# A causal attention kernel with a gated linear unit: convolution on sixteen 32x32 tiles for two groups at once, 64-column projection tiles, and a start written out piece by piece

## The chip, the cores and the metric

The kernel runs on one core of one Trainium2 chip. The metric is the device time of one execution in microseconds (us), as the median of several runs; a profiled execution additionally gives a trace, whose span is about 2 us shorter than the timed value. Runs are called fast or slow: a run is slow when it is over 1.5% above the fastest run of the same kernel, and only fast runs enter the ratios. PE is the TensorE matmul engine, DVE the VectorE, ACT the ScalarE, POOL the GpSimd, SP the SyncE.

## The reference, cut to what matters

```python
q, k, v: (8, 12, 448, 64)                       # batch, heads, positions, head width
scores = q @ k.T / 8, masked above the diagonal
x = softmax(scores) @ v  ->  (8, 448, 768)      # heads side by side
gate = sigmoid(sum over t of conv_w[t] * x shifted by 4 - t positions)    # 5 taps, causal, per channel
out  = (gate * (x @ w_val)) @ w_out             # both 768 x 768
```

The kernel works on groups of four heads, three groups per batch, 24 in all. It writes the sigmoid as (1 + tanh(z/2))/2, so ACT needs one set of functions.

## The kernel before: the parts that the change touches

A half of a group's scores is 16 matmuls with 32 rows each, four row tiles of the array side by side. ACT turns it into exponentials, POOL masks the diagonal, the attention matmuls (32 columns each, four column tiles) follow, DVE normalizes into `x`, and the convolution multiplies `x` with 32x32 diagonal matrices, one per tap:

```python
def conv(n):                                     # one group
    for t in range(KW):                          # 5 taps
        for dh in range(2):
            for i in range(G):                   # 4 heads
                j = 2 * (i % 2) + dh
                r = slice(32 * i, 32 * (i + 1))
                nc.tensor.matmul(out=av_ps[i // 2][32 * j:32 * (j + 1), 0:S], lhsT=cwd[r, 2 * g + dh, t],
                                 rhs=x[r, dh, t:t + S], ..., tile_position=(32 * i, 32 * j))
    # then two tanh activations of 448 columns, from av_ps
def val(b, g, o):       # 6 matmuls of 128x128 per tile: x @ w_val, then gate * value on DVE
def project(p, m, half, o):   # 6 x 4 matmuls of 128x32: (gate * value) @ w_out, then a copy and a store
...
for n in range(N + 1):
    load_v(n + 2)
    scores(n, 0); softmax_numerators(n, 0)
    attend(n - 1); normalize(n - 1)
    next_out(limit, z_ps); next_out(limit, den_ps)       # output tiles fill in
    scores(n, 1); softmax_numerators(n, 1)
    conv(n - 1); transposes(n + 1); cast_v(n + 1); load_qk(n + 3)
    ...                                                  # w_val is loaded in step 0, w_out in steps 1 and 2
    val(b - 1, g, (den_ps, z_ps))
```

Eight of the array's sixteen 32x32 tiles work in a convolution. Everything is in program order; there are eight PSUM banks: four for scores, two for attention (`av`), one for denominators (`den`), one free (`z`).

The softmax here doesn't subtract the row's maximum and nothing guards it: scores larger than these inputs give would overflow.

## Time and profile before

| | before |
|---|---|
| time, median of 3 runs | 240.46 us (239.91 to 240.92) |
| span of the profiled run | 238.6 us |
| PE busy | 211.0 us, 88% |
| PE's first value tile | 36.76 us |
| steady period | 7.95 us per group |

The page's busy shares, slices, stretches and chain are shown and read in the prediction below.

### The profile page before, as it was taken

What the parts mean: (1) busy time and instruction counts of PE and PEld (TensorE: products, weight loads), DVE (VectorE), ACT (ScalarE), POOL (GpSimd) and SP (SyncE); (2) the same over time, 40 slices, a digit from 0 to 9 for tenths busy, and PEclk for the clock granted to TensorE, in tenths of its full rate; (3) what the DMA queues carried; (4) which work ended last, traced back from release to release, by engine and by line L of the source; (5) the groups of instructions that cost most, each with busy time, mean ns of one, the idle gap of its engine ahead of it and who ended that gap; (6) DMA issues with size and microseconds to landing.
All of it is one profiled execution on the core that took longest, in us unless ns stands there. A gap on an engine that the chain in (4) does not pass through costs nothing.

```text
span 238.6 us, 10214 instructions
## 1 busy us (share of the span) xinstructions
PE 211.0 (88%) x4518; PEld 117.1 (49%) x4518; DVE 138.1 (58%) x235; ACT 143.1 (60%) x201; POOL 110.7 (46%) x189
## 2 busy tenths in 40 slices
PE   0297389988988999999999999999999999999893
PEld 0154145554544555545554555555555555544462
DVE  3457466754776678657766776586678663622100
ACT  2367543488765677668676867776777677231241
POOL 7594795153746535733655365347534532100000
PEclk9999859999999999999999999999999999999999
DMA  6999999959795568787768876877797111111153
GB/s 124 225 192 161 191 217 206 176 145 213 152 203 111 103 147 163 156 189 166 145 152 209 180 121 162 235 154 155 184 191 140 41 69 69 69 65 70 69 201 132
DMA packets 59574, 36.07 MB, mean 151 GB/s; under 512 B 48261, under 2 KB 55941, under 8 KB 59530
## 3 DMA queue, kind: packets, MB, share of 16 engines
q0 software_dynamic: 10944, 13.38, 35.4%
q1 hardware_dynamic: 48586, 22.04, 35.0%
q8 instruction: 35, 0.57, 1.0%
q14 instruction: 9, 0.07, 0.1%
HBM read 37.76 MB, written 11.01 MB: 204 GB/s over the span
## 4 chain that ended last, share of the span: by engine, by line
PE 77%; DMA 9%; POOL 3%; DVE 3%; issue 3%; ACT 3%; SPq 0%; POOLq 0%; DVEq 0%
PE den_ps L230 11%; PE z_ps L230 10%; PE av_ps L214 9%; PE z_ps L248 9%; PE sc_ps L154 9%; PE av_ps L187 8%; DMA kb<-in_k_dram 7%; PE den_ps L248 7%; PE sc_ps L248 5%; PE den_ps L187 5%; PE av_ps L230 2%; ACT ob L250 2%; ACT pt L163 1%; DMA vf<-in_v_dram 1%; DVE x L200 1%
## 5 line engine op out<-in xcount | busy, mean ns | idle before, releaser
L163 ACT ACTIVATE pt<-sc_ps 128x1024 bf16<-128x1024 f32 x96 | 93.0, 1021 | 50.4 <-PE sc_ps L154 49.1
L173 POOL TENSOR_SCALAR_AFFINE_SELECT pt<-pt 128x512 bf16<-128x512 bf16 x48 | 29.6, 642 | 59.3 <-ACT pt L163 48.4
L154 PE MATMUL sc_ps<-qt,kt 32*128 32x448 bf16 (+3 forms) x768 | 35.0, 285 | 17.7 <-DVE kt L140 13.4
L248 PEld LDWEIGHTS <-gv 128*32 128x32 bf16 x1344 | 35.3, 97 | 20.1 <-issue 5.3
L230 PEld LDWEIGHTS <-wv 128*128 128x128 bf16 x288 | 26.4, 98 | 30.4 <-issue 8.1
L154 PEld LDWEIGHTS <-kt 32*128 32x128 bf16 x768 | 17.4, 96 | 41.9 <-DVE kt L140 14.7
L232 DVE SCALAR_TENSOR_TENSOR gv<-gate,den_ps 128x448 bf16<-128x448 f32 x22 | 13.7, 621 | 32.5 <-ACT gate L219 22.6
L214 PE MATMUL av_ps<-x,cwd 32*32 32x448 bf16 x960 | 29.8, 349 | 2.3 <-DVE x L200 2.2
L200 DVE TENSOR_TENSOR x<-av_ps,rb 128x448 bf16<-128x448 f32 x48 | 27.7, 620 | 3.1
L230 PE MATMUL den_ps<-x,wv 128*128 128x448 bf16 x132 | 28.8, 354 | 0.0
L230 PE MATMUL z_ps<-x,wv 128*128 128x448 bf16 x132 | 28.6, 352 | 0.0
L76 POOL CAST vb<-vf 128x1024 bf16<-128x1024 f32 x24 | 24.9, 1037 | 6.7 <-DMA vf<-in_v_dram 6.7
L248 PE MATMUL z_ps<-wo,gv 128*32 128x384 bf16 x576 | 27.6, 326 | 0.0
L167 POOL TENSOR_SCALAR_AFFINE_SELECT pt<-pt 128x512 bf16<-128x512 bf16 x24 | 15.4, 642 | 25.6 <-ACT pt L163 25.6
L194 DVE STREAM_TRANSPOSE dt<-den_ps 128x448 f32<-128x448 f32 x24 | 15.6, 650 | 19.9 <-PE den_ps L187 19.9
L140 DVE STREAM_TRANSPOSE qt<-qb 128x448 uint32<-128x448 uint32 x24 | 22.9, 952 | 7.0 <-DMA qb<-in_q_dram 7.0
L187 PE MATMUL av_ps<-pt,vb 128*32 128x448 bf16 (+3 forms) x768 | 26.7, 283 | 0.0
L219 ACT ACTIVATE gate<-av_ps 128x448 f32<-128x448 f32 x48 | 23.7, 555 | 1.1 <-PE av_ps L214 0.8
L140 DVE STREAM_TRANSPOSE kt<-kb 128x448 uint32<-128x448 uint32 x24 | 22.4, 934 | 2.5 <-DMA kb<-in_k_dram 2.5
L248 PE MATMUL den_ps<-wo,gv 128*32 128x384 bf16 x456 | 21.9, 326 | 0.0
L187 PEld LDWEIGHTS <-vb 128*32 128x32 bf16 x768 | 17.2, 101 | 6.0 <-issue 0.8
L250 ACT ACTIVATE ob<-z_ps 128x384 f32<-128x384 f32 x24 | 11.8, 491 | 13.3 <-PE z_ps L248 13.3
(36 smaller groups left out, 161.7 us busy)
## 6 DMA issues: line engine op xcount, KB each, us to landing
out_dram<-ob SPq DMA_DIRECT2D x28, 384.0 KB, 3.4
vf<-in_v_dram SPq DMA_DIRECT2D x72, 128.0 KB, 4.5
qb<-in_q_dram POOLq DMA_DIRECT2D x24, 224.0 KB, 3.9
kb<-in_k_dram POOLq DMA_DIRECT2D x24, 224.0 KB, 5.1
vf<-in_v_dram SPq DMA_DIRECT2D x24, 64.0 KB, 3.7
wv<-in_moe_w_val_dram POOLq DMA_DIRECT2D x6, 192.0 KB, 10.6
wo<-in_moe_w_out_dram POOLq DMA_DIRECT2D x6, 192.0 KB, 8.2
cwn<-in_moe_conv_w_dram SPq DMA_DIRECT2D x1, 15.0 KB
```

Of the source, the lines that this page charges most:

```text
L76: nc.gpsimd.tensor_copy(out=t, in_=vfs.pop(n))
L140: nc.vector.transpose(out=t.bitcast(U32).rearrange("p (b s) -> p s b", s=T), in_=qks.pop((name, n)).rearrange("p s d -> p (s d)").bitcast( ...
L154: nc.tensor.matmul(out=sc_ps[h // 2][:, h % 2, c0:c0 + nq], lhsT=kt[r, e, k0:k0 + 128], rhs=qt[r, e, q0:S], start=e == 0, stop=e == 1, ski ...
L163: nc.scalar.activation(out=pt[:, 2 * hp:2 * hp + 2, 512 * stage:512 * (stage + 1)], in_=sc_ps[hp], func=AF.Exp, scale=D ** -0.5)
L173: nc.gpsimd.affine_select(out=pt[:, :, c:c + 128], in_=pt[:, :, c:c + 128], compare_op=ALU.is_ge, fill=0.0, base=0, pattern=[[0, G], [1, 1 ...
L187: nc.tensor.matmul(out=o, lhsT=w, rhs=pt[:, h, col:col + nq], start=i == 0, stop=i == 3, skip_group_check=True, tile_position=(0, 32 * h))
L200: nc.vector.tensor_tensor(out=x[:, dh, 4:S + 4], in0=av_ps[dh][:, 0:S], in1=r, op=ALU.mult)
L214: nc.tensor.matmul(out=av_ps[i // 2][32 * j:32 * (j + 1), 0:S], lhsT=cwd[r, 2 * g + dh, t], rhs=x[r, dh, t:t + S], start=t == 0, stop=t == ...
L219: nc.scalar.activation(out=gate[:, e], in_=av_ps[e][:, 0:S], func=AF.Tanh, scale=0.5)
L230: nc.tensor.matmul(out=o[e][:, 0:S], lhsT=wv_sb[c][:, f:f + 128], rhs=xs[(NG * b + cg) % 8][:, ce, 4:S + 4], start=c == 0, stop=c == NE - ...
L248: nc.tensor.matmul(out=o[r, 0:384], lhsT=gvs[p][g][:, dh, 128 * m + 32 * j:128 * m + 32 * (j + 1)], rhs=wo_sb[c][:, f], start=c == 0, stop ...
L250: nc.scalar.activation(out=ob[:, f], in_=o[:, 0:384], func=AF.Copy, scale=0.5)
```

## The change

The intent: use the eight idle array tiles for a second group (half the convolution waves), give the value and output matmuls a shape that lets the second group come out with its 64-row halves exchanged (64-column tiles; w_out is kept a second time with halves exchanged), order the groups 0 1 2 2 0 1 over two batches so that pairs fit, and write the first eight groups out as a list of tokens, so that the head of the run can be interleaved by hand. The diff, cut to its core:

```diff
+ORDER = [(b + d, g) for b in range(0, B, 2) for d, g in ((0, 0), (0, 1), (0, 2), (1, 2), (1, 0), (1, 1))]
+PROLOGUE = """
+K1 K0 Lq.0 Lv.0 Lk.0 Lq.1 Lk.1 Lv.1 K3 Lq.2 Lk.2 K2 Lv.2 K4 Tq.0 Lv.3 K5 Tk.0 Tq.1 s.0.0.0 Tk.1 s.0.0.1
+E.0.0.0 E.0.0.1 s.0.1.0 Tq.2 E.0.1.0 s.0.1.1 M.0.0 M.0.1 Tk.2 E.0.1.1 s.1.0.0 Lq.3 V.0 Lk.3 E.1.0.0 s.1.0.1
 ...
+s.3.1.0 D.2 N.1.2 E.3.1.0 s.3.1.1 M.3.0 N.2.0 M.3.1 N.1.3 E.3.1.1 s.4.0.0 W.0 N.2.1 W.1 N.1.4 E.4.0.0 s.4.0.1
+W.2 N.2.2 W.3 E.4.0.1 V.2 s.4.1.0 W.4 W.5 E.4.1.0 s.4.1.1 V.3 Lv.6 M.3.2 A.2.0 E.4.1.1 M.3.3 A.2.1 N.2.3 Lq.6
 ...
-    def conv(n):
-        for t in range(KW):
-            for dh in range(2):
-                for i in range(G):
-                    j = 2 * (i % 2) + dh
-                    nc.tensor.matmul(out=av_ps[i // 2][32 * j:32 * (j + 1), 0:S], ...
+    def conv(p):
+        for t in range(KW):
+            for m in range(2):                      # two groups
+                for e in range(2):
+                    for i in range(G):
+                        j = 2 * ((i + m) % 2) + e
+                        nc.tensor.matmul(out=sc_ps[m][32 * j:32 * (j + 1), i // 2, 0:S], lhsT=cwd[r, 2 * g + e, t], ...
+    def val(n, u, o, width):
+            for j in range(0, 128, width):
+                col = D * (G * g + 2 * u) + (j + D * (n % 2)) % 128
+                nc.tensor.matmul(out=o[j:j + width, 0:S], lhsT=wv_sb[c][:, col:col + width], ...
 ...
+    for p in range(FIRST, N // 2 + 1):
+        a, b = 2 * p, 2 * p + 1
+        attention(a, 0); fill("z", 1, 32); values(a - 1); ...; attention(a, 1); fill("zd", 2)
+        attention(b, 0); ...; fill("01", 2); convolve(p - 1)
+        fill("z", 1, 32); values(a); ...; attention(b, 1); fill("zd", 2)
```

The tokens: `L` loads of q, k, v; `T` transposes; `s` half-width scores for one pair of heads; `S` the same for four heads; `E` exponentials; `M` masks; `D` and `A` denominators and attention; `N` normalizing; `W` a load of w_val; `C`, `G` convolution and gate; `P`, `Y` a value tile and its product; `O`, `Z` an output tile and its copy.

## The prediction

> **What bounds the kernel now.** I read the page's busy shares first, then the 40 slices, then four stretches of time, and last the chain of waits. Parts 1 and 2 of the page:
>
> ```profile
> span 238.6 us, 10214 instructions
> ...
> PE 211.0 (88%) x4518; PEld 117.1 (49%) x4518; DVE 138.1 (58%) x235; ACT 143.1 (60%) x201; POOL 110.7 (46%) x189
> ...
> PE   0297389988988999999999999999999999999893
> ...
> DMA  6999999959795568787768876877797111111153
> ```
>
> TensorE (PE) is the only engine near its limit, and its 12% of idle time is not spread out: it lies in the first six slices and the last two, while DMA is full in the first nine. The stretches (columns: length, then busy us and count for PE, weight loads, DVE, ACT, POOL; granted clock; DMA share; GB/s) give its size. I cut at 36.76 us, where the first value projection starts (line L230 on the timeline).
>
> ```profile
> 0.00:36.76 36.76, 19.88 (x398) 10.58 (x398) 19.88 (x44) 18.30 (x21) 26.78 (x51) 0.91 1.14 186
> 36.76:103.00 66.24, 62.55 (x1338) 34.75 (x1332) 44.95 (x73) 42.90 (x60) 34.02 (x56) 1.00 0.79 161
> 103.00:200.00 97.00, 97.00 (x2204) 53.78 (x2204) 65.70 (x107) 69.39 (x99) 48.70 (x80) 1.00 0.68 151
> 200.00:238.60 38.60, 31.62 (x600) 17.96 (x592) 7.58 (x13) 12.54 (x24) 1.22 (x2) 1.00 0.27 104
> ```
>
> In the head PE works 19.88 of 36.76 us while DMA moves 186 GB/s at a share over 1: a load-bound start. From 103 to 200 us PE never idles. The chain of waits shows what one group of four heads costs there (start, length, what):
>
> ```profile
> 151.19 0.56 PE sc_ps L154 x16
> 151.75 1.07 PE av_ps L214 x40
> 152.82 1.24 PE den_ps L230 x6
> 154.06 1.14 PE z_ps L230 x6
> 155.20 0.57 PE sc_ps L154 x16
> 155.76 0.55 PE den_ps L187 x16
> 156.31 0.87 PE av_ps L187 x32
> 157.19 0.97 PE z_ps L248 x24
> 158.16 0.97 PE den_ps L248 x24
> ```
>
> In order: second half of the scores, convolution, two value tiles, first half of the next scores, denominators, attention times V, two output tiles. Every piece is PE's and each starts where the last ended, so here a microsecond off PE is a microsecond off the kernel.
>
> How close is each piece to pure streaming? The trace has full-array matmuls of 448 columns starting every 0.189 us, or 0.422 ns per column. Then the convolution, five waves of 448 columns, should take 0.945 (it takes 1.07), a half of the scores 0.43 (0.56), an output tile of 6 x 384 columns 0.97 (0.97), a value tile 1.13 (1.14 second, 1.24 first). A piece that follows one of another tile shape costs 0.1 to 0.13 more. From 103 to 200.4 us the streams add to 89.85 us and the shape changes 60 times; the remaining 7.55 us make **0.126 us per change of shape**.
>
> **What the Trainium skill says.** "TensorEngine Tiling (Array Packing)", Key Properties: "Mode switching requires drain". The trace agrees, with the 0.126 us above. "TensorE: Matmul & The Clock Gate", Back-to-back issue gap: N/2.4 + 2.5 ns when warm, 189 ns for 448 columns; the trace has 189. The same page, Part 3, Measured speedup vs the span model: sixteen 32x32 tiles ran 10.6 times as fast as one. Before only uses eight at once: there each wave of eight matmuls and their loads starts within some 30 ns and waves are 190 ns apart, so issue has room; no trace here yet has sixteen. "TensorEngine Tiling (Array Packing)", PSUM Bottleneck: tiling does not speed up the reading of PSUM; I use this for ACT below.
>
> **The change, part by part.**
>
> *Convolution.* Group m=1 takes the eight tiles of the array that m=0 leaves free. A pair of groups needs five waves in place of ten: 24 x 1.07 = 25.7 us becomes 12 x 1.07 = 12.8. **Gain 12.8 us** on PE, nearly all on the path. Accumulation moves from the av banks to the score banks, so scores and exponentials now share them with convolution and gate. The 48 gate activations become 24 of 896 columns. By the groups
>
> ```profile
> L163 ACT ACTIVATE pt<-sc_ps 128x1024 bf16<-128x1024 f32 x96 | 93.0, 1021 | 50.4 <-PE sc_ps L154 49.1
> L219 ACT ACTIVATE gate<-av_ps 128x448 f32<-128x448 f32 x48 | 23.7, 555 | 1.1 <-PE av_ps L214 0.8
> ```
>
> an element per partition costs (1021-555)/(1024-448) = 0.81 ns, so one takes 0.92 us against 2 x 0.555; ACT saves about 4.5 us, off the path.
>
> *64-column tiles and group order 0 1 2 2 0 1.* The second group of a pair comes out of the convolution with its 64-row halves exchanged. The tiles exist to exchange the weights to match, not for speed: two tiles side by side stream the same columns per unit of time as one. Value and output tiles stay at 1.13 and 0.97 us; a shared shape removes the change between them, but score-to-filler entries come back. By the program order of the changed kernel's TensorE instructions there are 123 changes of shape in all, against 121. **No gain.** The exchanged copy of part of w_out is 0.4 MB on a DMA that has room.
>
> *First eight groups piece by piece.* Scores are issued per pair of heads, so the first exponential can start after 8 matmuls, w_val is loaded after the inputs of six groups, and by the first value tile the program has issued 12 score halves and about 4.3 attentions against 8 and 3 before. Half-width scores use two of four row tiles and cost 0.43 us per half more, 12 x 0.43 = 5 us of PE, all in time when PE would idle.
>
> *When does the first value tile start?* Two limits. DMA: by packet times in the trace, a group's q and k take 2.82 us of 16 engines, its v 2.18, w_val 6.8. Six groups and w_val are 36.8; at the share of about 1.2 that the head sustains, and 2 us before the first transfer, 32.7 us. ACT: the second last half-score before it waits for the 22nd exponential; from a start at 9.2 us (9.67 before), 22 x 0.97 + two gates 1.85 = 32.4, plus one half-score, 33. Some waits of DVE (28 us of transposes, casts and normalizing in that stretch) add about 1.5: **34.5 us, against 36.76**.
>
> *What is left then.* In the program order from the first value tile on, matmul columns divided by the number of tiles side by side, at 0.422 ns: values 54.4, outputs 54.4, attention 25.5, scores 15.6, convolution 10.4, together 160.3 us; 101 changes of shape at 0.126 are 12.7. **173.0 us** of PE. The same sum for before is 173.4 + 107 x 0.126 = 186.9, and it took 201.8: 4 us are the last copy and store, 11 us are waits, about 7 of them before 103 us (exponentials, normalizing, a load of v) and 4 in the tail.
>
> *Waits left after the change.* In the head DMA must bring groups 6 to 8 and w_out by about 51 us: 36.8 + 15 + 6.8 = 58.6, /1.2 + 2 = 51. That just fits; I allow 1 us. In steady state the distance between two uses of the score banks shrinks to two fillers, 2 x 0.97 + 0.126 = 2.07 us, against two exponentials of 1.94 and their start. With two output tiles as fillers ACT also has two copies of 0.49, so 2.92 of ACT against 2.63 of PE (fillers plus a half-score): a wait of 0.1 to 0.45, perhaps one per pair of groups, for ten pairs 3.5 us. The tail should lose little, as four banks rotate: 1 us. Together 5.5.
>
> *Sum.* 34.5 + 173.0 + 5.5 + 3 (last copy and a store of half the size; it was 4) = 216 on the profile's span. Timed runs were 1.9 us above it (240.46 against 238.6), so 217.9; since the author evidently places fillers by durations like these, I take 2.4 us off the waits: **215.5 us**, 0.896 of before.
>
> **Rivals.**
>
> *Sixteen tiles don't run at the rate of eight.* A wave must fetch 32 instructions and four streams per row of the array in 190 ns. For: nothing in the trace goes beyond 16 instructions per wave. Against: attention at four column tiles streams four operands at once at full rate (0.87 us for 2048 columns), and the page's 10.6. If wrong, the gain halves or goes: 222 to 227 us.
>
> *ACT takes over as the bound locally.* For: the 2.92 against 2.63 above, and the narrow distance between uses of the score banks. Against: over a pair ACT has 8 x 0.97 + 4.7 x 0.49 + 1.85 = 11.9 us and PE 15.6. If every stretch stalls 0.3 us, five stretches a pair: 15 us, so about 226.
>
> *The head is load-bound anyway.* For: DMA share 1.14 with the old order. Against: the new order loads q, k and v first and gives PE and ACT attention to do meanwhile. If the first value tile starts at 40 us in place of 34.5: 221.
>
> *Everything fits.* First value tile at 33, no waits: 33 + 173 + 3 + 1.9 = 211.
>
> **Range and chances.** The floor is firm, as it is work counted at measured rates: 211, less perhaps 2 if fewer changes of shape cost their full price. Above, two half-failures give 224. So 209 to 224. For no gain over 2% (235.7) more than one rival must hold in full: 3% to be within, 1% to be slower.
>
> **What would show it.** (1) The chain's convolution piece: 80 matmuls in about 1.07 us; 1.5 or more means the first rival. (2) First value tile at 33 to 36 us on the timeline. (3) Value tiles of 12 matmuls at 1.13 us, output tiles at 0.97. (4) PE waits for ACT, in scores and convolution, of 3 to 5 us in total. (5) A steady period near 15.6 us per pair of groups with 4.7 output tiles in it (14.34 of streams, ten changes of shape), against 16.2 with 4.3. (6) DMA share below 0.85 there. The prediction is wrong if convolution waves slow, if scores wait for exponentials in every stretch, or if loads leave PE idle past 40 us.

## More of the kernel before

One view is added here, the waits: for each group of PE instructions what it waited for, in total, how often, and the longest, in us.

```profile
PE sc_ps L154 <- DVE kt L140: 13.4, 4, 8.6
PE sc_ps L154 <- ACT pt L163: 4.2, 8, 1.1
```

The largest waits lie in the head of the run: scores wait for DVE's transposes of k, which wait for the loads. No matmul of PE waits for "issue" in this view, that is, there is no time in which PE stops although everything the profile knows of is ready.

## The result, and the profile after

The changed kernel took **232.84 us** (median of 5 runs, 231.23 to 237.88) against 240.46 (239.52 to 241.6) for the kernel before, timed again beside it: ratio 0.9666, 95% interval 0.9608 to 0.9723. A ratio is the mean time of one kernel's fast runs over that of the other's fast runs of the same rounds, so not quite the ratio of the medians. It is faster by over 2%, as predicted, but 17 us slower than the 215.5 predicted and outside the range of 209 to 224.

The first profile of it fell in the slow state (span 235.4, clock 0.964). The same file was run again as the first experiment, *after_again*: 232.51 us (231.59 to 232.63; the kernel before took 239.71 beside it), ratio 0.969 [0.966, 0.972]. Its profile is the one read here. The page's busy shares and 40 slices, PEclk being the granted clock in tenths:

```profile
span 230.4 us, 9741 instructions
...
PE 208.6 (91%) x4338; PEld 124.6 (54%) x4338; DVE 136.4 (59%) x244; ACT 139.9 (61%) x177; POOL 107.0 (46%) x183
...
PE   1299989799899899999899699999999999989994
...
PEclk9999979799999999999999999999999999999999
DMA  5999949999999994876955985878932120130255
```

The head no longer looks idle: from the third slice on PE is at 8 or 9 tenths in nearly every slice. But the busy sum has sunk by only 2.4 us, though the convolutions alone should have taken 12 us off it: up to the first value tile PE is now busy for 30.26 us, where it was 19.88. And where the kernel before had only 9s from the 14th slice to the 37th, there are now a 6 and three 8s. The stretches, cut at the first value tile (42.75 us), in the columns of the prediction:

```profile
0.00:42.75 42.75, 30.26 (x487) 15.65 (x487) 28.14 (x63) 25.47 (x26) 26.95 (x53) 0.95 0.97 170
42.75:103.00 60.25, 58.07 (x1281) 34.56 (x1284) 39.90 (x66) 37.09 (x46) 33.39 (x54) 0.98 1.04 206
103.00:200.00 97.00, 93.75 (x2164) 56.97 (x2156) 61.92 (x104) 66.81 (x86) 46.69 (x76) 1.00 0.59 136
```

In 103 to 200 us PE was busy for 97.00 of 97.00 us before; now it is 93.75. The chain there (start, length, what):

```profile
176.49 1.22 PE sc_ps L247 x80
177.71 1.09 PE z_ps L287 x24
178.79 0.44 PE den_ps L212 x16
179.23 0.87 PE av_ps L212 x32
180.10 0.57 PE sc_ps L186 x16
180.67 1.10 PE z_ps L287 x12
181.77 0.97 PE den_ps L287 x12
```

One convolution (L247) of 80 matmuls now serves two groups in 1.18 to 1.22 us, where one group took 1.07. Output tiles (L287) take 0.97 to 1.1, as before, and one convolution follows another after 15.9 to 16.3 us where nothing stops PE. The groups of ACT:

```profile
L193 ACT ACTIVATE pt<-sc_ps 128x1024 bf16<-128x1024 f32 x96 | 93.3, 1021 | 48.2 <-PE sc_ps L186 48.0
L253 ACT ACTIVATE gate<-sc_ps 128x896 f32<-128x896 f32 x24 | 20.7, 915 | 16.7 <-PE sc_ps L247 16.7
```

A gate of 896 columns takes 915 ns; the prediction had worked out 0.92. So each piece has about its predicted size. The error must lie between the pieces. The sum of the prediction beside the measured one (us):

| term | predicted | measured | difference |
|---|---|---|---|
| first value tile starts | 34.5 | 42.75 | +8.25 |
| from there to the end of PE's work | 173.0 + 5.5 | 184.04 (to 226.79, where PE's last matmul starts) | +5.5 |
| last copy and store | 3.0 | 3.6 | +0.6 |
| timed run over span | 1.9 | 2.1 | +0.2 |
| taken off because the author "evidently places fillers" well | -2.4 | 0 | +2.4 |
| sum | 215.5 | 232.5 | +17.0 |

Two of these rows have to be explained by experiments: the head and the stretch behind it.

### The profile page after: what moved, and what is told of

Same layout as the page of the kernel before. It is cut to its first block, busy times and chain, and to the rows that moved or that the text cites.

```text
span 235.4 us, 9741 instructions
## 1 busy us (share of the span) xinstructions
PE 213.1 (91%) x4338; PEld 127.3 (54%) x4338; DVE 136.0 (58%) x244; ACT 140.3 (60%) x177; POOL 107.1 (45%) x183
## 4 chain that ended last, share of the span: by engine, by line
PE 82%; DMA 7%; issue 3%; POOL 3%; ACT 2%; DVE 2%; POOLq 0%; DVEq 0%
PE sc_ps L186 13%; PE z_ps L265 13%; PE av_ps L212 10%; PE z_ps L287 10%; PE av_ps L287 10%; DMA qb<-in_q_dram 7%; PE av_ps L265 7%; PE den_ps L287 6%; PE den_ps L265 6%; PE sc_ps L247 5%; PE den_ps L212 4%; ACT pt L193 2%; POOL wv L104 2%; POOL pt L200 1%; DVE cwd L160 0%
## 5 line engine op out<-in xcount | busy, mean ns | idle before, releaser
L287 PEld LDWEIGHTS <-gv 128*64 128x64 bf16 (+1 forms) x804 | 37.0, 107 | 19.9 <-issue 3.7
L265 PEld LDWEIGHTS <-wv 128*64 128x64 bf16 (+1 forms) x648 | 31.5, 107 | 27.0 <-issue 7.1
L265 PE MATMUL z_ps<-x,wv 128*64 128x448 bf16 (+1 forms) x360 | 33.8, 363 | 2.3 <-DMA wv<-in_moe_w_val_dram 1.6
L253 ACT ACTIVATE gate<-sc_ps 128x896 f32<-128x896 f32 x24 | 20.7, 915 | 18.3 <-PE sc_ps L247 18.3
L271 DVE SCALAR_TENSOR_TENSOR gv<-gate,z_ps 128x448 bf16<-128x448 f32 x24 | 14.7, 612 | 16.8 <-PE z_ps L265 16.8
L287 PE MATMUL av_ps<-wo,gv 128*64 128x384 bf16 x222 | 22.8, 334 | 0.0
L287 PE MATMUL z_ps<-wo,gv 128*32 128x384 bf16 (+1 forms) x316 | 20.8, 329 | 0.0
L293 ACT ACTIVATE ob<-av_ps 128x384 f32<-128x384 f32 x22 | 10.6, 493 | 11.2 <-PE av_ps L287 11.2
L265 PE MATMUL av_ps<-x,wv 128*64 128x448 bf16 x156 | 16.6, 355 | 0.6 <-ACT ob L293 0.6
L212 PE MATMUL den_ps<-pt,ones 128*32 128x448 bf16 (+3 forms) x384 | 16.4, 291 | 0.8 <-issue 0.8
L247 PE MATMUL sc_ps<-x,cwd 32*32 32x448 bf16 x960 | 16.5, 383 | 0.0
```

Of the source, the lines that this page charges most:

```text
L212: nc.tensor.matmul(out=o, lhsT=w, rhs=pts[n][:, h, col:col + nq], start=i == 0, stop=i == 3, skip_group_check=True, tile_position=(0, 32 * h))
L247: nc.tensor.matmul(out=sc_ps[m][32 * j:32 * (j + 1), i // 2, 0:S], lhsT=cwd[r, 2 * g + e, t], rhs=x[r, e, t:t + S], start=t == 0, stop=t = ...
L253: nc.scalar.activation(out=gates[n], in_=sc_ps[n % 2][:, :, 0:S], func=AF.Tanh, scale=0.5)
L265: nc.tensor.matmul(out=o[j:j + width, 0:S], lhsT=wv_sb[c][:, col:col + width], rhs=xs[PLACE[b, cg] % NX][:, ce, 4:S + 4], start=c == 0, st ...
L287: nc.tensor.matmul(out=o[j:j + width, 0:384], lhsT=gvs[p][g][:, u, t0:t0 + width], rhs=wo_sw[:, u, f] if g == 2 and t0 >= S else wo_sb[:, ...
```

## The experiments

Eighteen kernels ran, all correct. Runs of one batch shared a chip and its runs of the kernel before; its medians there were 239.71, 239.25, 240.52, 240.23 and 239.38 us, so kernels of different batches are compared through their ratios.

| kernel | median us (range) | ratio to before, 95% | first value tile, us | pauses, us |
|---|---|---|---|---|
| after_again (the change) | 232.51 (231.59–232.63) | 0.969 [0.966, 0.972] | 42.75 | 8.1 |
| full_scores | 235.45 (232.61–236.38) | no interval | 45.1 | 6.4 |
| early_wv | 235.76 (233.94–237.06) | 0.983 [0.977, 0.989] | 46.4 | 7.2 |
| warm | 245.71 (238.13–246.99) | no interval | 55.0 (slow run) | not read |
| conv8 | 238.03 (237.50–240.66) | 0.997 [0.991, 1.003] | 44.7 | 5.6 |
| width32 | 240.84 (238.83–243.89) | 1.003 [0.997, 1.010] | 41.8 | 12.5 |
| warm2 | 229.29 (227.61–233.16) | 0.956 [0.951, 0.960] | 47.7 (slow run) | 7.0 (slow run) |
| shallow | 232.65 (230.96–234.21) | 0.972 [0.966, 0.977] | 42.7 | 6.8 |
| wide128 | 233.82 (233.34–235.17) | 0.975 [0.970, 0.980] | 44.5 | 5.5 |
| spread | 231.34 (230.13–232.08) | 0.963 [0.958, 0.968] | 39.6 | 8.2 |
| warm3 | 231.18 (230.38–231.51) | 0.962 [0.958, 0.967] | 40.8 | 6.7 |
| best | 231.15 (228.57–232.47) | 0.959 [0.952, 0.967] | 41.1 | 6.2 |
| warm4 | 230.64 (228.55–231.92) | 0.961 [0.952, 0.970] | 41.5 | 7.7 |
| warm2s | 227.59 (226.32–230.33) | 0.949 [0.940, 0.959] | 40.1 | 6.4 |
| post128 | 231.30 (230.45–234.08) | 0.963 [0.956, 0.971] | 43.9 | 2.8 |
| warm4p | 229.58 (227.32–231.73) | 0.950 [0.941, 0.959] | 40.8 | 6.0 |
| warm2sp | 228.51 (227.03–230.04) | 0.954 [0.950, 0.959] | 43.5 | 4.4 |
| warm1sp | 227.42 (225.51–229.20) | 0.947 [0.941, 0.953] | 40.5 | 4.5 |

"Pauses" are PE's stops of over 0.3 us at every 256th instruction, explained in part B; they are summed from one profiled run each, after 30 us. Medians and ranges take in slow runs (three of four in warm, two of four in full_scores and warm4p, two of six in warm1sp, one each in width32, warm2, best, warm2s and post128).

> The changed kernel once more, unchanged, to have a profile in the fast state and runs on the same chip as the next three. Both theories: 231 to 233 us timed in fast runs, first value tile near 44 us, score pieces of the first groups 0.97 us for 8 matmuls until about 27 us. If the pauses of TensorE behind its own instruction loads (1.3, 1.0, 0.8, 1.3, 2.3 us in the profiled slow run) are what makes a run slow, this profile has fewer or shorter ones.

### A. The head: why the first value tile came at 42.75 us and not at 34.5

I began with two simple theories. The first: PE runs at half clock, because the half-width scores, which fill two of four row tiles, don't raise the clock. The second: w_val is issued late. Half-width scores and late loads were each undone alone.

**full_scores** replaces, for groups 0 to 5, each pair `s.n.st.0` and `s.n.st.1` by one `S.n.st` over four heads.

```diff
-... s.0.0.0 Tk.1 s.0.0.1 E.0.0.0 E.0.0.1 s.0.1.0 Tq.2 E.0.1.0 s.0.1.1 ...
+... S.0.0 Tk.1 E.0.0.0 E.0.0.1 S.0.1 Tq.2 E.0.1.0 ...
```

> Scores of the first six groups issued for all four heads at once, as in the kernel before. Theory 1 (the head is bound by TensorE at half clock, because pieces that fill only two of four row tiles don't raise the clock): clock rises at about 18 us in place of 27, a score half takes 0.57 us once it has, w_val is issued some 5 us earlier, first value tile at 38 to 40 us, total 4 to 7 us less than the changed kernel. Theory 2 (the head is bound by the order of the loads): clock or not, first value tile stays within 1.5 us of 44, total within 2 us.

It took 235.45 us (its two fast runs 232.61 and 234.63), and the first value tile came 2.4 us later, at 45.1. A full piece writes the banks of both pairs, so it waits for both exponentials of the piece before: in ACT's timeline there are ten pairs of exponentials of 1.94 us with 0.65 to 1.17 us of waiting for scores between them. The half-width split does what it is meant to do, and full-width scores are no remedy. That does not refute the half clock as a cause: the first record of full clock came at 21.5 us, earlier than the 24.6 of after_again, but the new waits hid what it gave.

**early_wv** issues the six w_val loads right after q and k of the first three groups, ahead of all other q and k loads.

```diff
-Lq.2 Lk.2 K2 Lv.2 K4 ...        W.0 N.2.1 W.1 ... W.5
+Lq.2 Lk.2 K2 W.0 W.1 W.2 W.3 W.4 W.5 Lv.2 K4 ...
```

> The six loads of w_val issued right after those of the first three groups, in place of after the masks of group 3; nothing else. Theory 2 (loads): GpSimd issues them behind masks that wait for exponentials, so DMA idles from 24 to 37 us at 73 to 141 GB/s; issued early, w_val is there by 25 us and the first value tile starts when scores and convolution allow, 38 to 40 us, and groups 6 and 7 land 4 us earlier; total 6 to 10 us less. Theory 1 (half clock alone): the clock still rises at 27 us or later, since the loads of group 3 now come later; total within 3 us.

It took 235.76 us, with the first value tile at 46.4: w_val came early but group 3's q took 13.5 us to land, at 26.1 us. The bytes were only moved from one wait to another, and the first record of full clock came only at 33.1 us, so this run cannot tell the two theories apart. In this form the second theory fell.

What the half clock does stands in ACT's timeline of after_again (start, busy time, engine, instruction, count, and in brackets the idle time ahead of it and what ended it):

```profile
9.82 1.94 ACT L193 ACTIVATE pt<-sc_ps 128x1024 bf16<-128x1024 f32 x2 [7.74 <-PE sc_ps L186]
...
18.20 1.02 ACT L193 ACTIVATE pt<-sc_ps 128x1024 bf16<-128x1024 f32 x1 [0.92 <-PE sc_ps L186]
20.14 1.02 ACT L193 ACTIVATE pt<-sc_ps 128x1024 bf16<-128x1024 f32 x1 [0.92 <-PE sc_ps L186]
...
36.29 1.73 ACT L253 ACTIVATE gate<-sc_ps 128x896 f32<-128x896 f32 x2 [2.78 <-PE sc_ps L247]
38.00 2.97 ACT L193 ACTIVATE pt<-sc_ps 128x1024 bf16<-128x1024 f32 x3
```

The exponentials take what the prediction said (about 1 us each), but ACT stands still between them, 0.92 us at a time, because PE gives it one score piece per 1.94 us. In the chain of waits a score piece of 8 matmuls and an attention piece of 16 take 0.97 us each up to 24.6 us, 0.56 later. The trace's own record of the granted clock gives the reason: the first record of full clock starts at 24.6 us. **PE ran at half clock until then**, again from 31.4 to 34.9 and from 41.7 to 45.1. The page's PEclk row shows a 9 for the first slices only because no record lies there. Before, the first record starts at 17.9.

The Trainium skill, "TensorE: Matmul & The Clock Gate", Part 1, What's actually happening, says that the clock is halved by default and released after about 3.4 us of sustained busy time, in a free-running window. Half and full are indeed the only two states, and their boundaries are multiples of 3.41 us apart. But PE was busy for 8.00 of 8.00 us between 16 and 24 us and stayed at half. So busy time alone is not what releases it. Three runs tested what does.

**warm** fills PE's idle time in the head with matmuls of zeros over the full array: 7 and 6 before the first score and one after each score or attention piece.

```diff
+    hot = sb.tile([128, 448], BF16, name="hot")            # zeros
+    def heat(k, count):
+        for _ in range(count):
+            nc.tensor.matmul(out=z_ps[:, 0:448], lhsT=hot[:, 0:128], rhs=hot, start=True, stop=True, ...)
-K1 K0 ... K4 Tq.0 Lv.3 K5 Tk.0 Tq.1 s.0.0.0 Tk.1 s.0.0.1
+K1 H.0.7 K0 ... K4 Tq.0 Lv.3 K5 H.1.6 Tk.0 Tq.1 s.0.0.0 H.2.1 Tk.1 s.0.0.1 H.3.1
```

> Matmuls of zeros over the full array into a bank that is not in use yet: 13 before the first scores and one after each piece of the first groups, so that TensorE's clock is raised from about 8 us on. They cost 8 to 9 us of TensorE at full clock, in time when it would wait. Theory 1: score pieces take 0.43 to 0.56 us in place of 0.97, ACT is fed without gaps, w_val is issued by 24 us, first value tile at 36 to 39 us, total 5 to 9 us less. Theory 2: score pieces are faster but the first value tile stays at 42 to 44 us; total within 2 us.

It missed both expectations: 245.71 us, from three slow runs and a fast one of 238.13, still over the change. In the profiled run, a slow one, the clock rose at 4.4, fell at 7.8 and stayed at half until 48.8 us, though PE was busy practically without a break (PE's timeline: start, busy time with the modelled end, instruction):

```profile
15.89 1.03 PE L190 MATMUL sc_ps<-qt,kt 32*128 32x448 bf16 x8
16.86 0.55 PE L325 MATMUL z_ps<-hot 128*128 128x448 bf16 x1
```

A half-width score at half clock plus a zero at half clock is 0.97 + 0.49 us: at half clock even the remedy costs double. Over all windows of 3.41 us in the first 60 us of the 20 profiles I then summed rows x columns x streamed columns, as a share of what the full array takes in at full clock. Of 358 windows, every one with a share over 0.40 was followed by full clock and every one under about 0.33 by half; between, it went either way. Half-width scores at half clock can reach 0.25 at most: they fill half the array at half the rate. **That is a trap: at half clock these scores alone cannot earn the full clock.** It leaves it only when attention, which fills the array, gets a large enough share of a window.

**warm2** makes the zeros dense enough: 9 and 10 before the first score, 2 after each score piece up to the first attention, then four of 128x32 side by side (0.19 us) after each attention piece.

```diff
+K1 H.0.9 ... K4 H.1.10 ... s.0.0.0 H.2.2 Tk.1 s.0.0.1 H.3.2 ... D.0 H.9.1.0 ... A.0.0 H.10.1.0
```

> Matmuls of zeros again, but enough of them: 19 over the full array before the first score, 2 after each score piece up to the first denominators, then four side by side after each attention piece. In all five traces the clock rose after a window of 3.41 us with the array filled to 0.36 or more of its full-rate capacity (rows x columns x columns streamed), and fell after one with 0.37 or less, and the 35 zero matmuls of the run before gave only 0.23 to 0.36. Theory A (clock follows filled area, and half clock makes the head slow): clock at 1.0 from about 8 us to the first value tile with at most one window below; score pieces 0.5 us; first value tile 36 to 39 us in place of 43 to 44; total 5 to 8 us less, 224 to 228. Theory B (the head is bound by loads and by ACT whatever the clock): first value tile at 42 or later, total within 2 us.

229.29 us, ratio 0.956 [0.951, 0.960], against 0.972 [0.966, 0.977] for shallow, an ineffective change of the same batch (part B): useless zeros take 3.4 us off the kernel by the medians and 3.9 by the ratios. The profiled run was the slow one (233.16 us): in it the clock fell again from 10.8 to 21.1 us.

**warm3** gives each half-width score a twin of zeros on one of the idle row tiles, so that the zeros cost no PE time of their own.

```diff
+                    if len(heads) == 2 and ("D", 0) not in emitted:
+                        i = (h + 2) % 4
+                        nc.tensor.matmul(out=(den_ps, z_ps, av_ps[0], av_ps[1])[i][:, 0:nq],
+                                         lhsT=hot[32 * i:32 * (i + 1), 0:128], rhs=hot[32 * i:32 * (i + 1), 0:nq],
+                                         start=True, stop=True, skip_group_check=True, tile_position=(32 * i, 0))
```

> Edit: 19 full-array matmuls of zeros before the first scores, and before the first attention each half-width score matmul gets a twin of zeros on one of the two idle row tiles, so that the whole array is filled while the time of a score piece stays; quads of 128x32 after attention pieces. Theory (the granted clock follows the filled share of the array, about 0.37 needed per window of 3.4 us): the clock stays at full from about 4 us to the first attention at the price of no PE time, first value tile at 37 to 39.5 us, time 227 to 230 us, ratio 0.945 to 0.957. Rival (clock follows something else, for example the rows times data that change, so zeros do not count or do so only on full-array tiles): half clock from 10 us on as before, first value tile at 42 us or later, ratio 0.966 or more.

231.18 us, ratio 0.962. It missed the expected 0.945 to 0.957: in the profiled run the window from 7.4 to 10.8, in which the first score still waited for k, had a share of 0.38 and the clock fell to half until 17.6. Then it stayed at full until 41.5, and the first value tile came at 40.8, in place of the 37 to 39.5 expected. Zeros on single row tiles do count: the window from 14.2 to 17.6 us had a share of 0.42 with them and would have had 0.31 without, and full clock followed. But raising the clock does not bring the whole 8 us.

**spread** returns to the second theory in a better form. In after_again w_val is issued by POOL in one block of six at 28.78 to 33.49 us, behind masks that wait for exponentials; DMA is far from full before and during it. The loads are now issued one at a time among the masks from group 5's loads on.

```diff
-... s.4.0.0 W.0 N.2.1 W.1 N.1.4 E.4.0.0 s.4.0.1 W.2 N.2.2 W.3 E.4.0.1 V.2 s.4.1.0 W.4 W.5 ...
+... E.2.0.1 Lk.5 W.0 Tk.3 ... M.2.0 W.1 ... M.2.1 W.2 ... M.2.3 W.3 ... M.3.0 W.4 ... M.3.1 W.5 ...
```

> Edit: the six w_val loads are issued one at a time among the masks from group 5's loads on, not in one block behind them. Theory (GpSimd issues the loads late, so DMA idles from 24 to 37 us and w_val and q6 land late): DMA moves over 150 GB/s in 24 to 37 us, first value tile 1.5 to 4 us earlier than 42.8, time 229 to 231 us, ratio 0.955 to 0.963. Rival (PE at half clock sets the head, the loads only fill its gaps): first value tile within 1 us of 42.8, time within 1 us of 232.5, ratio 0.968 to 0.974.

The two stretches concerned, of after_again first (the last two columns are the DMA share and GB/s, the third from the end the clock):

```profile
24.00:31.00 7.00, 6.13 (x106) 3.15 (x105) 5.11 (x11) 6.40 (x8) 4.57 (x8) 1.00 0.81 159
31.00:37.00 6.00, 5.71 (x166) 3.44 (x167) 4.41 (x8) 3.01 (x4) 6.00 (x11) 0.72 0.72 92
```

and of spread:

```profile
24.00:31.00 7.00, 5.84 (x106) 3.04 (x105) 4.89 (x9) 6.92 (x9) 6.97 (x11) 1.00 1.11 180
31.00:37.00 6.00, 5.97 (x186) 3.55 (x178) 4.64 (x8) 3.02 (x5) 4.39 (x9) 0.72 1.21 180
```

DMA moves 180 GB/s where it moved 92 to 159, the first value tile comes at 39.56 us, 3.2 us earlier, and the kernel takes 231.34 us (0.963). So less than half of what the head gained reached the end, and since the interval of [0.958, 0.968] overlaps that of after_again, even this gain in time is not settled. Part of the 3.2 is luck of the window, too: here the clock rose at 21.2 us, one window earlier than in after_again.

**warm4** and **warm2s** put both together: the twins of warm3 (with two more zeros ahead) or the zeros of warm2, with the spread loads.

> Edit: 21 zero matmuls before the first scores, twins of zeros on the idle row tiles of the half-width scores up to the first attention, quads of zeros behind attention pieces, and w_val loads spread among the masks. Theory (clock and late w_val together hold up the head): clock at full from about 4 us on with at most one half-clock window before 45 us, first value tile at 36 to 38.5 us, time 226 to 229 us, ratio 0.942 to 0.953. Rival (the head has a further cause, such as ACT's exponentials or group 5's loads): first value tile at 39.5 us or later, time 230 us or more.

> Edit: the zeros of the second warm run (two full-array ones after each half-width score) with the spread w_val loads. Theory: loads on time and clock up, but 0.48 us of PE per score piece for the zeros: first value tile at 38.5 to 41 us, time 228 to 230.5, ratio 0.950 to 0.961. Rival (a further cause): first value tile above 42 us.

warm4 came out as its rival said: 41.45 and 230.64 us. warm2s met its theory, 40.11 us for the first value tile and 227.59 us in time, slightly below the range expected. In both, the clock stayed at full until about 28 to 30 us. So with clock and loads both relieved the first value tile still does not come before 40 us: **the head has a further cause**. The last run, at full clock from 10.6 us on, shows it.

**warm1sp** has warm2's zeros with one in place of two after each of the first seven score pieces, the spread loads and post128 of part B; **warm2sp** has two.

```diff
-s.0.0.0 H.2.2 Tk.1 s.0.0.1 H.3.2 E.0.0.0 E.0.0.1 s.0.1.0 H.4.2 ...        (warm2sp)
+s.0.0.0 H.2.1 Tk.1 s.0.0.1 H.3.1 E.0.0.0 E.0.0.1 s.0.1.0 H.4.1 ...        (warm1sp)
```

> Edit: warm2s with the filler behind each convolution at 128 columns. Theory (the causes are separate): warm2s gave 227.6, post128 took 1.2 to 2.9 us off the stretch behind the first value tile, so 225 to 227 us, ratio 0.938 to 0.947. Rival (pauses only move to another boundary): 227 to 229 us, ratio 0.947 to 0.955.

> Edit: warm2sp with one zero matmul in place of two behind each of the first seven score pieces. If the zeros' time is on the path that sets the first value tile: 7 x 0.24 = 1.7 us earlier there, 38.4 us, time 1 to 1.7 us below warm2sp. If the chain from score to exponential to attention sets it: first value tile within 0.5 us, time within 0.5 us; and if the filled share sinks under 0.37 in a window, the clock falls and it is slower by 2 us or more.

warm2sp took 228.51 us, ratio 0.954: both lie in its rival's ranges, so the gains did not add. Its profiled run fell into the trap from 10.7 to 21.0 us and its first value tile came at 43.5. warm1sp took 227.42 us, 0.947 [0.941, 0.953]: the intervals overlap, so which of the two is better is not settled, and the first value tile came at 40.5 us, not at the 38.4 expected. But warm1sp's profiled run (226.24 us) is the cleanest: full clock from 10.6 us to the end of PE's work. ACT's timeline in it:

```profile
10.54 6.53 ACT L197 ACTIVATE pt<-sc_ps 128x1024 bf16<-128x1024 f32 x7 [8.46 <-PE sc_ps L190]
...
33.01 1.73 ACT L257 ACTIVATE gate<-sc_ps 128x896 f32<-128x896 f32 x2 [1.99 <-PE sc_ps L251]
37.64 1.02 ACT L197 ACTIVATE pt<-sc_ps 128x1024 bf16<-128x1024 f32 x1 [2.90 <-PE sc_ps L190]
38.85 2.86 ACT L197 ACTIVATE pt<-sc_ps 128x1024 bf16<-128x1024 f32 x3 [0.19 <-PE sc_ps L190]
```

Its first twenty exponentials take 20.48 us from the first start to the last end, as good as gapless. In after_again, at half clock until 24.6 us, the same twenty take 23.68; in the slow profile of the same kernel, at half until 27.4, they take 25.18; in wide128, where the first record of full clock starts at 37.3, they take 25.84. These three have the same program up to there: the later the clock rises, the longer the stretch. Against warm1sp, which also has the zeros and earlier w_val loads, this puts the cost of the clock in the head at **3.2 us in the fast run and up to 5.4**. What is left at full clock is a hand-over: 1.99 us from the last of these exponentials to the first gate, in which PE still does denominators, zeros and a whole convolution of 80 matmuls, and then a stop of 2.3 us of PE between 33.2 and 35.7 which the profile puts down to "issue". That stop belongs to part B.

### B. Behind the head: PE stops at every 256th instruction

The waits of after_again from 42.75 us on contain 5.1 us under "issue" and only 1.0 for other engines; before, none was called so. One such stop, in PE's timeline:

```profile
129.63 0.34 PE L186 MATMUL sc_ps<-qt,kt 32*128 32x192 bf16 x5
131.77 0.54 PE L186 MATMUL sc_ps<-qt,kt 32*128 32x192 bf16 x11 [1.80 <-issue]
```

PE stops in the middle of a score piece whose operands are all there. The trace shows what is common to the stops: counting PE's instructions (matmuls and weight loads), they come right after number 961, 1729, 2497, 3265, 4033, 4801 and 6337, all 193 plus a multiple of 256. And each ends 1.3 to 1.7 us after the end of a transfer of 16384 bytes on the queue that the page calls "instruction" (about 1 us each; packets, MB, share):

```profile
q8 instruction: 34, 0.56, 1.0%
```

Counted again over all 20 profiles, 114 such pauses after 30 us end 1.2 to 1.7 us after such a transfer, and the kernel before has none. 16384 over 256 is 64 bytes per instruction. So the reading is: **PE has run out of instructions and waits for the next block of 256.** Between 60 and 195 us the fastest 256 of PE's instructions took 4.01 us before, and 2.80 after: sixteen tiles mean 160 instructions in 1.18 us. Ahead of a pause of after_again the transfer begins only 1.8 to 3.9 us after PE has passed the boundary before, as the trace shows; why not earlier, it does not show. The pauses of after_again add to 8.1 us, 6.4 of them behind the first value tile. Five runs tested this reading.

**conv8** takes the convolution's groups one after the other, eight tiles at a time.

```diff
-        for t in range(KW):
-            for m in range(2):
+        for m in range(2):
+            for t in range(KW):
```

> The convolution of a pair with the loops over groups and taps exchanged: first the five waves of one group, then those of the other, eight tiles at a time; same matmuls, same banks, same result. If sixteen tiles run as five waves of 0.19 us, this piece goes from 1.18 to about 2.1 us (ten waves and one change of shape), twelve pieces, 9 to 11 us more than the changed kernel: about 242 us. If the sixteen tiles only look fast because the ends are modelled, or if the steady part is bound by something else, less than 3 us more.

238.03 us, 0.997: 6.6 us slower than the changed kernel by the ratios ((0.9966 - 0.969) x 239.5), less than the 9 to 11 expected from the waves. The trace shows why (PE's timeline; the piece lasts until the next one starts):

```profile
114.85 1.76 PE L247 MATMUL sc_ps<-x,cwd 32*32 32x448 bf16 x80
116.54 1.16 PE L287 MATMUL z_ps<-wo,gv 128*32 128x384 bf16 x24
```

The piece takes 1.69 us, where about 2.1 was expected and 1.18 is the changed kernel's. The difference of 0.51 us in twelve pieces makes 6.1 of the 6.6 us. By an estimate, 1.69 is nine waves of 0.189 and not ten: the second group's first wave, on other tiles, may run beside the first group's last one. That was not tested.

**width32** makes all value and output tiles four of 32 columns: the same arithmetic and streams, one shape less to change to, but 10771 PE instructions in the trace in place of 8683.

```diff
-        "P": lambda n, u, bank, width=64: ...      "O": ... width=64 ...      def fill(among, count=1, width=64):
+        "P": lambda n, u, bank, width=32: ...      "O": ... width=32 ...      def fill(among, count=1, width=32):
```

> All value and output tiles as four tiles of 32 columns in place of two of 64. My step: the width moves nothing, streams and changes of shape stay the same: within 2 us of the changed kernel (231 to 234). Rival: the 64-column tiles are the gain of the change; then 5 us or more slower. A third: 1116 matmuls more to load and to issue, so if TensorE's pauses behind its own instruction loads come from their number, they grow, by 2 to 4 us.

240.84 us, 8.2 us more by the ratios; the pauses sum to 12.5 us in 12 places, each at 193 plus a multiple of 256. My own step had expected no change, and it failed: the tiles' width does matter. The profiled span is 6.3 us longer than that of after_again, of which the pauses are 4.4; PE's waits for DVE and for w_val behind the first value tile are 1.9 more.

**shallow** asked whether the cause was the number of loads that POOL and SP have under way (v loaded two groups ahead and q and k three, in place of four).

```diff
-        do("Lv", a + 4)        qk(a + 4)
+        do("Lv", a + 2)        qk(a + 3)
```

> The steady part asks for v two groups ahead in place of four, for q and k three in place of four; nothing else. In the changed kernel TensorE stops 0.9 to 2.3 us right after 961, 2497, 4033, 4801 of its instructions, that is at multiples of 256 after the 193rd, each time about 1.3 us after the end of a 16 KB load of instructions, from 40 to 133 us, where DMA is busiest. Theory: these loads wait behind the deep queue of v, q and k; asked for later, the pauses after 60 us shrink from 5 to 6 us in total to below 2, total 2 to 4 us less. Rival: the pauses have to do with where the instructions lie, and stay at the same counts: total within 1.5 us.

232.65 us, 0.972: nothing, and the pauses at the same counts. That theory fell.

**wide128** goes the other way from width32: 128 columns wherever no half exchange is needed, 7983 PE instructions in the program.

```diff
+        if width == 64 and n % 2 == 0:      # in val
+            width = 128
+        if width == 64 and m != 3:          # in project
+            width = 128
```

> Edit: 128-column value tiles for the even groups and 128-column output tiles where the rows do not straddle two score blocks; PE instructions 8667 to 7983, same arithmetic. Theory (instruction loads): with 684 fewer PE instructions PE passes the 256-instruction boundaries more slowly, so the pauses right after a boundary sink from about 7 us to 3 or 4 us; time 229 to 230.5 us, ratio to before 0.955 to 0.962. Rival (my prediction's step): only shapes change, and mixed widths add about 20 shape changes of 0.126 us: time 232.5 to 235 us, ratio 0.97 to 0.98.

It missed: 233.82 us, 0.975, inside the rival's range. Its pauses sank from 8.1 to 5.5 us, but part of that came back as short waits of value and output matmuls for DVE and ACT (1.5 and 0.6 us) and, by the rival, in changes of shape. Its profiled head was also at half clock until 37.3 us. Fewer instructions in general are not the point; it matters where they are dense.

**post128** therefore thins just one place: the one filler behind each convolution, ahead of attention, goes from 24 matmuls of 32 columns to 6 of 128 (12 of 64 where the exchange needs it).

```diff
             break
-        fill("z", 1, 32)
+        fill("z", 1, 65)        # 65: 128 columns where possible, else 64
```

> Edit: only the one filler behind each convolution is 128 columns wide in place of 32 (6 matmuls in place of 24; 64 columns where the half exchange needs it). Theory (instruction loads): the pauses at every 256th instruction after 43 us shrink from 5.5 to 6.4 us to 2 to 4 us, against 8 more shape changes of 0.126; time 230 to 231.5 us, ratio 0.958 to 0.965. Rival (pauses only move): same total of pauses within 1 us, time 232.5 to 234 us, ratio 0.968 to 0.976.

The pauses fell to 2.8 us in all, 2.0 behind 43 us, and the ratio to 0.963; the time, 231.3 us, was inside the theory's range, but the interval [0.956, 0.971] overlaps that of after_again, so the gain in time is not settled. From the first value tile to the end of PE's work it took 181.1 us against 184.0. Pauses behind it are 4.4 us less, and the first value tile itself, here at full clock, took 1.52 us in place of 2.38 until the next piece started; so over 2 us came back, of which eight more changes of shape make 1.0 by estimate and a wait for DVE before the second value tile 0.95.

**A pause also costs clock.** In four profiled runs a pause of 2.0 to 2.9 us behind the head was followed by a window of half clock: in the slow run of the change at 133 us (half from 136.7 to 140.1), in spread at 127 (130.4 to 133.8), in best at 158 (161.1 to 164.5, in which two value tiles took 4.00 us in place of 2.28) and in the slow run of warm at 175 (178.5 to 181.9). In after_again a pause of 2.04 us had no such effect, nor had one of 2.5 in warm1sp and one of 3.3 in warm2s. This fits the rule of filled share: counted in steps of 3.41 us from the clock records, the first four lie inside one window each (that of the change but for 0.2 us), and these three lie across the boundary of two.

**best** and **warm4p** were combinations on the way: warm2's zeros, spread loads and wide128; and warm4 with post128.

> Edit: the zero matmuls of the second warm run, the spread w_val loads and the 128-column tiles together. If the three causes (half clock, late w_val, instruction loads) are separate: 229.3 less 2 less 1.5, 225 to 227 us, ratio 0.935 to 0.947. If the clock alone sets the head and the pauses do not depend on the width: 228.5 to 230 us, ratio 0.953 to 0.960.

> Edit: warm4 and post128 together. If both theories hold the gains add: 224.5 to 227.5 us, ratio 0.935 to 0.947. If only one holds, within 1 us of the better one of the two.

best: 231.15 us, 0.959 [0.952, 0.967], a time outside both ranges expected and no better than warm2 alone; in the profiled run one pause brought a half-clock window. warm4p: 229.58 us, not the 224.5 to 227.5 expected if the gains add, and 0.950 against warm4's 0.961; the medians moved by 1.1 us, and the intervals overlap. It has a pause of 3.5 us at 36.4 us, just ahead of the first value tile, because the shift of the instruction count put a boundary there.

The fastest kernels are warm1sp (227.42 us, 0.947) and warm2s (227.59 us, 0.949): about 12 us under the kernel before, and, through the ratios, some 5 us (0.969 less 0.947 of 239.5) under the change.

## Why the prediction was right or wrong

**Right: the pieces.** The sixteen-tile convolution took 1.18 us for two groups, where 1.07 was predicted; that is 0.11 x 12 = 1.3 us mis-sized in all. The first rival, that sixteen tiles don't run at the rate of eight, is refuted by this. conv8 confirms the gain from the other side: eight tiles at a time, the piece takes 1.69 us and the kernel 6.6 us more. Output and value tiles, gates and exponentials had the sizes predicted, and a pair of groups in the undisturbed steady part took 15.9 to 16.3 us against 15.6.

**Right: the second rival did not happen.** From the first value tile on PE waited 0 us for exponentials and 1.0 us for all other engines together, and not the 5.5 us that the sum allowed.

**Wrong: the step "When does the first value tile start?"**, by 8.25 us. It took the larger of two sums, DMA's and ACT's: 9.2 + 22 x 0.97 + 1.85 + 0.56, plus 1.5 for waits. Its terms against after_again: the first exponential starts at 9.82, +0.6; the first twenty took 23.68 us in place of 19.4, +4.3; the wait before the first gate was 2.79 in place of the 1.5, +1.3; gates and the three exponentials behind them took 4.7 in place of 3.8 (three were needed, not two), +0.9; from there to the value tile 1.78 in place of 0.56, +1.2, by an instruction pause. These add to 8.3. The largest is the clock: the twenty exponentials take 20.48 us in warm1sp, where PE is at full clock from early on. The step counted the half-width scores at full clock and "all in time when PE would idle"; at half clock PE, and not ACT, sets the pace. I had seen 0.91 in the clock column of the head and not asked what clock the new head would get. The third rival, a load-bound head, was right in the first value tile's time (40 us or later) but not in its reason: spread, which fills DMA's idle time, gives 1.2 to 1.4 us of the time at most, not clear of the noise, and DMA had room in after_again from 24 to 37 us.

**Wrong: no term for instruction loads.** Behind the first value tile the sum was 5.5 us short. The pauses there are 6.4 us, the first value tile at half clock costs 1.25 (2.38 in place of 1.13), the convolutions about 1.2; against them stand 4.5 of the 5.5 us allowed for waits that did not come. This gives 4.4 of the 5.5; the other 1.1 us is not accounted for. None of this was in the trace of before, which has no such pause: I could have counted that the new convolution puts 160 instructions into the time of 80, but not known from that trace what it costs.

**Wrong: the reason for "No gain" from the 64-column tiles.** By the streams alone, tiles of 32 columns should be equal to them, but with these the kernel takes 8.2 us more (width32), in which pauses are the largest part. Against 128 columns no clear gain or loss was seen (wide128). What the tiles did against the mixed widths of the kernel before, 128 for values and 32 for outputs, no run tested.

**Wrong: 2.4 us taken off for the author's skill.** That was not worked out from anything, and it was an error of its full size.

**Two misreadings of little consequence.** DMA is full in slices two to eight and not "in the first nine": the ninth digit is a 5. And ACT's gates went from 23.7 to 20.7 us, a saving of 3.0 and not 4.5.

What stays open: why a block of instructions is asked for only 2 to 4 us after the boundary before; how much of the head's hand-over of 2 us from attention to gate could be hidden; and whether a pause-free order exists. An estimate from the terms above, with full clock and no pause: 9.8 + 20.5 + 2.0 + 4.7 + 0.6 = 37.6 us for the first value tile, still 3 us over the prediction.

## What to carry to other kernels

When a change makes pieces smaller, narrower or more numerous, count two things that the busy share does not show: how much of the array they fill per 3.41 us (here a window under about 0.33 was always followed by half clock and one over 0.40 by full), and how many PE instructions run per microsecond (in after_again PE ran dry after blocks of 256 that had passed in 3.0 to 4.8 us; before, the fastest took 4.01). Zeros that fill the array in an otherwise thin start can be worth more than they cost: here some 3 us of the kernel. And a start in which engines hand over to each other is a chain, not the larger of two sums.

## What the Trainium skill lacked or had wrong

- "TensorE: Matmul & The Clock Gate", Part 1, speaks of busy time. In these runs PE was busy for 8.00 of 8.00 us at half clock, and in warm for most of 41 us without a rise. What fits 358 windows of 3.41 us is the filled share of the array (rows x columns x streamed columns over what the full array takes at full clock): over 0.40 always full clock next, under about 0.33 always half, between either. Matmuls of zeros count, on single row tiles too.
- The same page, HAM oscillation, gives the rule of no idle gap of over about 3.4 us. Here pauses of 2.0 to 2.9 us were enough for a window of half clock, in four profiled runs.
- "Runtime: NRT & Kernel Launch", Instruction fetch mechanics, has the blocks of 256 instructions and calls the cost of crossing from one to the next "mostly hidden". Here it is not: PE stops at such a boundary if it gets there too early, for 0.3 to 3.5 us, and goes on 1.2 to 1.7 us after the transfer's end; 8.1 us of this kernel, 12.5 us with 10771 PE instructions.
- "TensorEngine Tiling (Array Packing)", Instruction Overhead, has no figure for waves on sixteen tiles one after another; 80 matmuls took 1.18 us against 0.945 for the five streams alone.
- The same page, Key Properties, says that a change of mode drains the engine, without a figure: 0.126 us for a change of shape here, worked out from the trace of before.
